# The last block's last matrix product in column halves, on top of product 6's bank; one of its sums on ScalarE and GpSimd

## Chip, cores and metric

One core of one Trainium2 chip runs the whole program. The metric is device time in microseconds (us). The kernel before takes 217.72 us, the median of three runs (217.53 to 218.18).

## What is computed

```python
scores = (1 / sqrt(64)) * q @ k.T            # batch 4, heads 8, 768 positions, head size 64
keep   = (pos_k < 4) | (0 <= pos_q - pos_k < 128)   # 4 sink positions and a window of 128
a      = softmax(where(keep, scores, -1e9))
x      = (a @ v).reshape(3072, 512)          # tokens x model
h      = x @ w_in                            # 512 -> 2048
g      = h * sigmoid(1.702 * h)
out    = g @ w_out                           # 2048 -> 512, float32, 3072 x 512
```

## The kernel before

The 3072 tokens are worked in 12 blocks of 256 (`k` = 0 to 11, `NK` = 12). For each block TensorE makes the attention scores, ScalarE their exponentials, VectorE the mask and the normalised rows; then `mm1` (from line 824) multiplies by `w_in` (line 843), ScalarE takes a tanh (line 857) and VectorE makes `gT` from it (line 859). The last matrix product of a block is in `mm2_seven` (from line 880). It runs for blocks 1 to 11 and replaces the eight products of a 2 by 2 split (128 tokens, half of the 2048, 256 output columns) by seven, with sums of `gT` parts in `sm` (line 890) and of `w_out` parts in `wt` (line 873). Each product is eight matmuls of 256 columns, one for each 128 of its half of the 2048 (line 920).

The four output quarters are `c11`, `c12` (first 128 tokens, left and right 256 columns; tile `osb2` in the last block) and `c21`, `c22` (second 128 tokens; tile `osb3`). With P1 to P7 for the seven products, the sums are c11 = P1 + P2, c12 = P1 + P6 + P5 + P3, c21 = P1 + P7 + P4 + P6 and c22 = P1 + P7 + P6 + P5, each times 0.5. A product lands in a PSUM bank; where the next product is added to it in the bank, it runs with `start=False`. `read` (line 942) takes a bank out: on ScalarE as a copy times 0.5 (line 945), on VectorE as 0.5 times the bank plus an `osb` quarter (line 947).

The last block (`k == NK - 1`, lines 952 to 975) has its own order: P1 in bank a, copied by ScalarE to c12; P7 in bank e, added by VectorE to c22; P2 on top of P1, copied by ScalarE to c11; P4 on top of P7, added to c21; P6 in bank b, which VectorE reads three times (c12, c21, c22); P5 in bank d, read twice (c12, c22); P3 in a bank of its own, f, read once (c12). Each finished quarter leaves by a DMA of 128 KB from SyncE's queue (line 973): c11, c21, c22, c12.

The order is not that of the source. Every step is an `Op` with a cost, the steps that it depends on and a priority. `Plan.run` (line 70) goes through a model of the engines with these costs, and then writes the instructions out in the order of the planned starts. Semaphore waits are put in afterwards, from the tiles that an instruction reads and writes; for a PSUM bank such a wait can be for any earlier user of that bank. Each engine works its own instructions strictly in order.

Of the kernel before, what the change touches and what calls it, by code (L numbers as in the profile page):

```python
# [9 lines left out]
FP32 = mybir.dt.float32  # L10
FP16 = mybir.dt.float16
AF = mybir.ActivationFunctionType
ALU = mybir.AluOpType

P = 128
D = 64
TB = 256
# [37 lines left out]
class Plan:  # L55
# [4 lines left out]
    def op(self, eng, dur, lat, fn, deps=(), prio=0.0, acq=None, rel=(), kind=""):  # L60
        return self.any({eng: (dur, lat)}, lambda _: fn(), deps, prio, acq, rel, kind)
# [138 lines left out]
def pe_ns(n):  # L200
    return n / 2.4 + 2.5
# [3 lines left out]
def kernel(  # L205
# [11 lines left out]
    nc = tc.nc  # L217
# [28 lines left out]
    HM = d_model // 2  # L246
# [4 lines left out]
    def ring(name, n, shape, dt):  # L251
        return [pool.tile(list(shape), dt, name=f"{name}{i}") for i in range(n)]
# [19 lines left out]
    at = ring("at", RA, (P, 2, 512), FP16)  # L272
# [4 lines left out]
    th = ring("th", RTH, (P, 512), FP16)  # L277
    gT = ring("gT", RG, (P, NF, TB), FP16)
    sm = ring("sm", RSM, (P, 4, NH, P), FP16)
    osb = ring("osb", RO, (P, d_model), FP32)  # L280
# [3 lines left out]
    op = plan.op  # L284

    def f32(o, i=0):
        return bank[o.banks[i]]
# [21 lines left out]
    def uses(name, slot, o):  # L309
        users.setdefault((name, slot), []).append(o)  # L310

    def reuse(name, slot):

        return users.pop((name, slot), [])
# [23 lines left out]
    def keep_sinks():  # L338
# [9 lines left out]
        out=bias, in0=mask, scalar1=-1.0, scalar2=-OUT, op0=ALU.add, op1=ALU.mult), [o_mask], prio=MASK_AT, kind="mask")  # L348
# [8 lines left out]
    for b in range(B):  # L357
# [7 lines left out]
        prio = 24000.0 + 300.0 * b if b else NEVER + 0.5  # L365
# [46 lines left out]
    def nominal(k, slot):  # L412
        return 9000.0 + k * L + slot * L / 8
# [466 lines left out]
    def mm2_seven(k):  # L880


        g, X = gT[k % RG], sm[k % RSM]
        A = {"11": g[:, 0:NH, 0:P], "12": g[:, NH:NF, 0:P], "21": g[:, 0:NH, P:TB], "22": g[:, NH:NF, P:TB]}
        lo, hi = [o_g[k, s] for s in range(NS // 2)], [o_g[k, s] for s in range(NS // 2, NS)]
        war = reuse("sm", k % RSM)
        prio = nominal(k + 1, 0)

        def add(n, out, x, y, alu, deps):
            o = op("DVE", 595, 690, lambda: nc.vector.tensor_tensor(out=out, in0=x, in1=y, op=alu),  # L890
                   deps, prio=prio, kind="sum")
            uses("gT", k % RG, o)
            return o

        o1 = add("1", X[:, 0], A["21"], A["22"], ALU.add, lo + hi + war)
        o2 = add("2", X[:, 1], X[:, 0], A["11"], ALU.subtract, [o1] + war)
        o3 = add("3", X[:, 2], A["11"], A["21"], ALU.subtract, lo + war)
        o4 = add("4", X[:, 3], A["12"], X[:, 1], ALU.subtract, [o2] + war)
        S1, S2, S3, S4 = (X[:, n] for n in range(4))
        prod = {1: (A["11"], wq["11"], lo, None), 2: (A["12"], wq["21"], hi, None), 3: (S4, wq["22"], [o4], None),  # L900
                4: (A["22"], wt["4"], hi, "4"), 5: (S1, wt["1"], [o1], "1"), 6: (S2, wt["2"], [o2], "2"),
                7: (S3, wt["3"], [o3], "3")}
        O, wars = [], []
        for j in range(2):
            oi = n_o[0] % RO
            n_o[0] += 1
            O.append(oi)
            wars.append(reuse("osb", oi))
        T = [osb[oi] for oi in O]
        c11, c12, c21, c22 = T[0][:, 0:HM], T[0][:, HM:], T[1][:, 0:HM], T[1][:, HM:]  # L910
        last = {}

        def mm(n, slot, bank_of, first, after=()):

            x, w, deps, t = prod[n]
            for h in range(2):
                F0 = 4 * h
                def f(F0=F0, h=h):
                    for Fi in range(F0, F0 + 4):
                        nc.tensor.matmul(f32(holder[bank_of])[:, 0:HM], x[:, Fi], w[:, Fi],  # L920
                                         start=first and Fi == 0, stop=Fi == NH - 1,
                                         skip_group_check=True)
                d = list(deps) if t or n == 3 else deps[2 * h : 2 * h + 2]
                if k == SEVEN_FROM:
                    d = d + [*o_wout.values()]
                if t:
                    d = d + [o_wt[t, 2 * h], o_wt[t, 2 * h + 1]]
                d = d + list(after) + ([last[bank_of]] if bank_of in last else [])
                begin = first and h == 0
                o = op("PE", 4 * pe_ns(HM), 3 * pe_ns(HM) + HM / 2.4 + 166, f, d,  # L930
                       prio=nominal(k + 1, slot + h / 2 + -1) + 3, acq=("s" if k == NK - 1 else "o", 1) if begin else None,
                       kind="mm2")
                if begin:
                    holder[bank_of] = o
                last[bank_of] = o
                o_P[k, n, h] = o
                uses("gT", k % RG, o)
                uses("sm", k % RSM, o)

        holder = {}  # L940

        def read(eng, bank_of, out, add, deps, end, slot):
            src = lambda: f32(holder[bank_of])[:, 0:HM]
            if eng == "ACT":
                f, ns = (lambda: nc.scalar.mul(out, src(), 0.5)), (264, 380)  # L945
            else:
                f, ns = (lambda: nc.vector.scalar_tensor_tensor(  # L947
                    out=out, in0=src(), scalar=0.5, in1=add, op0=ALU.mult, op1=ALU.add)), (333, 425)
            return op(eng, *ns, f, [last[bank_of]] + deps, prio=nominal(k + 1, slot) + 3,
                      rel=[(holder[bank_of], 0)] if end else [], kind="read")  # L950

        if k == NK - 1:

            mm(1, 0, "a", True)
            r1 = read("ACT", "a", c12, None, wars[0], False, 1)
            mm(7, 1, "e", True)
            r7 = read("DVE", "e", c22, c12, [r1] + wars[1], False, 2)
            mm(2, 2, "a", False, [r1])
            ends = [(0, 0, read("ACT", "a", c11, None, wars[0], True, 3))]
            mm(4, 3, "e", False, [r7])  # L960
            r4 = read("DVE", "e", c21, c12, [r1] + wars[1], True, 4)
            mm(6, 4, "b", True)
            r6 = read("DVE", "b", c12, c12, [r4, r7], False, 5)
            ends.append((1, 0, read("DVE", "b", c21, c21, [r4], False, 5)))
            r26 = read("DVE", "b", c22, c22, [r7], True, 5)
            mm(5, 5, "d", True)
            ends.append((1, HM, read("DVE", "d", c22, c22, [r26], False, 6)))
            r5 = read("DVE", "d", c12, c12, [r6], True, 6)
            mm(3, 6, "f", True)
            ends.append((0, HM, read("DVE", "f", c12, c12, [r5], True, 7)))  # L970
            for j, c, after in ends:
                def f(j=j, c=c):
                    nc.sync.dma_start(out[k * TB + j * P : k * TB + j * P + P, c : c + HM], T[j][:, c : c + HM])
                uses("osb", O[j], op("SP", 500, (400.0,), f, [after], prio=nominal(k + 1, 7) + 4, kind="out"))
            return
        mm(1, 0, "a", True)
        r1 = read("ACT", "a", c21, None, wars[1], False, 1)
        mm(6, 1, "b", True)
        mm(2, 2, "a", False, [r1])
        r11 = read("ACT", "a", c11, None, wars[0], True, 3)  # L980
        r2 = read("DVE", "b", c12, c21, [r1] + wars[0], False, 2)
        mm(7, 3, "b", False, [r2])
        r3 = read("DVE", "b", c22, c21, [r1] + wars[1], False, 4)
        mm(5, 4, "d", True)
        mm(4, 5, "b", False, [r3])
        r22 = read("DVE", "d", c22, c22, [r3], False, 5)
        r21 = read("DVE", "b", c21, c21, [r1, r2, r3], True, 6)
        mm(3, 6, "d", False, [r22])
        r12 = read("DVE", "d", c12, c12, [r2], True, 7)
        prio = nominal(k + 1, 7) + 4  # L990
        for j, after in ((1, [r21, r22]), (0, [r11, r12])):
            rows = out[k * TB + j * P : k * TB + j * P + P, :]
            paired = rows.rearrange("(p i) f -> i p f", i=2)
            for i in range(2):
                def f(to=paired[i], fr=T[j][64 * i : 64 * i + 64], i=i):
                    nc.sync.dma_start(to, fr)
                o_d = op("SP", 500, (400.0,), f, after, prio=prio, kind="out")
                uses("osb", O[j], o_d)

    def mm2(k):  # L1000
        if SEVEN_FROM <= k < SEVEN_TO:
            return mm2_seven(k)
# [127 lines left out]
```

## Time and profile before

| | |
|---|---|
| time, median of three runs | 217.72 us (217.53 to 218.18) |
| time of the profiled execution | 218.23 us |
| its span, first to last instruction | 216.2 us |
| granted TensorE clock | 1.00 |
| TensorE busy | 210.8 us, 97% |
| VectorE busy | 185.4 us, 86% |
| ScalarE busy | 133.1 us, 62% |
| GpSimd busy | 86.0 us, 40% |
| last matmul ends | 213.09 us |
| last VectorE instruction ends | 213.55 us |
| last output bytes move | until about 214.97 us |

The profile is of one execution, so its times are compared with its own 218.23 us: 2.03 us of that lie outside the span. PE is TensorE's matmuls, PEld its weight loads, DVE VectorE, ACT ScalarE, POOL GpSimd, SP SyncE; SPq and ACTq are the sequencers that issue DMAs. Matmul ends are modelled. A row "x8" in the timeline is eight instructions of one group, from the start of the first to the end of the last.

### The profile page before, as it was taken

To read this page: it belongs to the slowest core of one execution; us is meant where nothing else is said; L and a number is where in the kernel's file an instruction comes from. 1 tells how busy PE (TensorE), PEld (TensorE's weight loads), DVE (VectorE), ACT (ScalarE), POOL (GpSimd) and SP (SyncE) were. 2 spreads that over 40 slices of the span, in tenths; PEclk is the share of its full clock that TensorE was granted. 3 is DMA by queue.
4 is the path that set the end of the run, shared out by engine and by line. 5 is a ranking of instruction groups with operands and counts; after the bars stand their busy time and mean duration, and the time that the engine had idled before them with its cause. 6 is when DMAs were issued, how large, how long until landed. Compare 5 with 4: busy or idle time off the path is not lost.

```text
span 216.2 us, 6592 instructions
## 1 busy us (share of the span) xinstructions
PE 210.8 (97%) x2680; PEld 181.0 (84%) x2680; DVE 185.4 (86%) x429; ACT 133.1 (62%) x277; POOL 86.0 (40%) x136
## 2 busy tenths in 40 slices
PE   7899999999999999999999999999999999999994
PEld 7568887678888988988888988888889889888883
DVE  5698899998988988988988979889979879878674
ACT  3867695366686775765675775864675865744330
POOL 7979564499996260699300080540000000000000
PEclk9999999999999999999999999999999999999999
DMA  6999999999999498099970099091040031022042
GB/s 179 215 196 179 200 192 205 168 163 166 108 167 165 30 144 77 5 133 170 89 124 3 0 96 125 5 114 36 3 97 3 0 76 28 0 52 49 2 100 97
DMA packets 79734, 21.41 MB, mean 99 GB/s; under 512 B 68184, under 2 KB 76888, under 8 KB 79704
## 3 DMA queue, kind: packets, MB, share of 16 engines
q0 software_dynamic: 71200, 12.59, 73.2%
q1 hardware_dynamic: 7416, 7.88, 13.5%
q10 hardware_dynamic: 1088, 0.52, 0.8%
q8 instruction: 21, 0.34, 0.7%
q14 instruction: 9, 0.07, 0.1%
HBM read 27.26 MB, written 6.29 MB: 155 GB/s over the span
## 4 chain that ended last, share of the span: by engine, by line
PE 92%; DVE 3%; DMA 2%; ACTq 1%; issue 0%
PE bank L843 39%; PE bank L920 31%; PE bank L695 5%; PE bank L775 5%; PE bank L1021 3%; DMA qk<-in_k_dram 2%; PE bank L618 2%; PE bank L770 2%; PE bank L585 2%; PE bank L555 1%; DVE osb L947 1%; PE bank L642 1%; PE bank L803 1%; ACTq L505 1%; PE bank L678 1%; DVE xn L792 1%
## 5 line engine op out<-in xcount | busy, mean ns | idle before, releaser
L843 PE MATMUL bank<-xT,w_in 128*128 128x256 f16 x768 | 103.7, 273 | 0.0
L857 ACT ACTIVATE th<-bank 128x512 f16<-128x512 f32 x96 | 57.6, 604 | 57.9 <-PE bank L843 51.6
L843 PEld LDWEIGHTS <-w_in 128*128 128x128 f16 x768 | 71.9, 98 | 8.9
L859 DVE SCALAR_TENSOR_TENSOR gT<-th,bank 128x512 f16<-128x512 f16 x96 | 64.9, 678 | 10.1 <-ACT th L857 9.8
L724 ACT ACTIVATE at<-bank 128x512 f16<-128x512 f32 (+1 forms) x96 | 49.1, 584 | 1.5 <-PE bank L695 1.1
L458 POOL DMA_DIRECT2D v<-in_v_dram x48 | 33.2, 719 | 30.4 <-PE bank L775 24.8
L920 PEld LDWEIGHTS <-sm 128*128 128x128 f16 x352 | 33.3, 98 | 4.2 <-issue 0.2
L920 PE MATMUL bank<-wt,sm 128*128 128x256 f16 x264 | 36.1, 273 | 0.0
L947 DVE SCALAR_TENSOR_TENSOR osb<-bank,osb 128x256 f32<-128x256 f32 x58 | 23.9, 417 | 11.8 <-PE bank L920 11.8
L920 PEld LDWEIGHTS <-gT 128*128 128x128 f16 x264 | 25.5, 98 | 3.4
L920 PE MATMUL bank<-w_out,gT 128*128 128x256 f16 x176 | 26.1, 273 | 0.0
L738 DVE TENSOR_TENSOR at<-at,mask 128x1024 f16<-128x1024 f16 x30 | 20.5, 683 | 0.2 <-ACT at L724 0.2
L792 DVE TENSOR_TENSOR xn<-bank,rcp 128x256 f16<-128x256 f32 x48 | 20.0, 417 | 0.6
L775 PE MATMUL bank<-v,at 128*128 128x65 f16 x352 | 20.0, 193 | 0.0
L434 POOL DMA_DIRECT2D qk<-in_q_dram x20 | 18.0, 925 | 0.6 <-DMA qk<-in_q_dram 0.5
L434 POOL DMA_DIRECT2D qk<-in_k_dram x20 | 18.0, 923 | 0.7 <-PE bank L843 0.5
L775 PEld LDWEIGHTS <-at 128*128 128x128 f16 x352 | 17.4, 97 | 0.9
L305 POOL COPY ks<-qkT 64x4 f16<-64x4 f16 x26 | 8.1, 313 | 18.6 <-DVE qkT L305 17.6
L890 DVE TENSOR_TENSOR sm<-gT 128x1024 f16<-128x1024 f16 x22 | 15.0, 680 | 0.1
L593 ACT ACTIVATE ats<-bank 128x256 f16<-128x256 f32 x32 | 13.0, 405 | 1.7 <-PE bank L585 1.6
L945 ACT ACTIVATE osb<-bank 128x256 f32<-128x256 f32 x22 | 8.4, 382 | 9.1 <-PE bank L920 9.1
L695 PE MATMUL bank<-qkT 64*128 64x256 f16 x192 | 13.3, 244 | 0.0
(58 smaller groups left out, 224.0 us busy)
## 6 DMA issues: line engine op xcount, KB each, us to landing
out_dram<-osb SPq DMA_DIRECT2D x48, 128.0 KB
v<-in_v_dram POOLq DMA_DIRECT2D x48, 64.0 KB, 5.1
qk<-in_q_dram POOLq DMA_DIRECT2D x20, 128.0 KB, 5.4
qk<-in_k_dram POOLq DMA_DIRECT2D x20, 128.0 KB, 5.6
w_out<-in_moe_w_out_dram POOLq DMA_DIRECT2D x4, 512.0 KB, 11.3
w_in<-in_moe_w_in_dram POOLq DMA_DIRECT2D x4, 256.0 KB, 6.6
w_in<-in_moe_w_in_dram POOLq DMA_DIRECT2D x2, 512.0 KB, 8.9
qk<-in_k_dram ACTq DMA_DIRECT2D x4, 128.0 KB
```

Of the source, the lines that this page charges most:

```text
L434: nc.gpsimd.dma_start(c16[:, i, e, hs], src[b, hs, t0 : t0 + TB].rearrange("h (p i) d -> i p h d", i=2)[i])
L458: o = op("POOL", ISSUE, (430 if k < 2 else V_NS,), lambda i=i, j=j, src=src: nc.gpsimd.dma_start(w16[64 * i : 64 * i + 64, j, :, 0:D], src ...
L695: nc.tensor.matmul(f32(o_b or o_s, 2 * n + i)[:, c : c + w].rearrange("s (j t) -> s j t", t=P), src[d, j, 1, p], T[d, j0:j1, 0, p], start= ...
L724: nc.scalar.activation(out=A[:, i, 0:W], in_=f32(o_b or o_s, 2 * n + i)[:, 0:W], func=AF.Exp, scale=scale)
L738: nc.vector.tensor_tensor(out=a_, in0=a_, in1=m_[:, 2 * P :].unsqueeze(1).to_broadcast((P, 4, 2 * P)), op=ALU.mult,)
L775: nc.tensor.matmul(avp()[:, j, i], A[:, i, c : c + P], src[:, jj, 2 * p + i, 0:E], start=not r and n == 0, stop=n == len(blocks) - 1, skip ...
L792: o_nn = op("DVE", 333, 425, lambda: nc.vector.tensor_tensor(out=X[:, p].rearrange("s j (h d) -> s j h d", h=2), in0=avp()[:, :, :, 0:D], ...
L843: nc.tensor.matmul(f32(holder[0])[:, bass.ts(e, TB)], w_in16[:, c, bass.ts(Fi, P)], X[:, c], start=(c == 0 and not (halved and e)), stop=( ...
L857: o_t = op("ACT", 477, 600, lambda first=first: nc.scalar.activation(out=th[first.places[0]], in_=f32(first), func=AF.Tanh, scale=0.851), ...
L859: o_g[k, s] = op("DVE", 595, 690, lambda first=first, s=s: nc.vector.scalar_tensor_tensor(out=g[:, 2 * s : 2 * s + 2].rearrange("p a t -> ...
L920: nc.tensor.matmul(f32(holder[bank_of])[:, 0:HM], x[:, Fi], w[:, Fi], start=first and Fi == 0, stop=Fi == NH - 1, skip_group_check=True)
L947: f, ns = (lambda: nc.vector.scalar_tensor_tensor(out=out, in0=src(), scalar=0.5, in1=add, op0=ALU.mult, op1=ALU.add)), (333, 425)
```

## The change

Only the last block changes. `mm` and `read` get a column offset `at` and a width `w_`.

- Bank b (P6) is read once by VectorE, for c21 (`r6`), and once by ScalarE, which copies it times 0.5 to a spare float32 tile in the space of `th0` (`r16`). GpSimd adds that tile to c22 (`a6`). The read of P6 into c12 is gone.
- VectorE reads bank d (P5) first into c12, then into c22; the second comes after GpSimd's add.
- P3 no longer has a bank. It runs on top of P6 in bank b, left 128 columns and then right 128 columns: sixteen matmuls of 128 columns in place of eight of 256. VectorE reads each half, 128 columns, into c12, which holds P1 + P5 by then.
- c12 leaves in two DMAs of 64 KB, the left half from ScalarE's queue and the right half from SyncE's.

```diff
-            r6 = read("DVE", "b", c12, c12, [r4, r7], False, 5)
-            ends.append((1, 0, read("DVE", "b", c21, c21, [r4], False, 5)))
-            r26 = read("DVE", "b", c22, c22, [r7], True, 5)
+            r6 = read("DVE", "b", c21, c21, [r4], False, 5)
+            ends.append((1, 0, HM, r6))
+
+            spare = th[0][:].bitcast(FP32)[:, 0:HM]
+            r16 = read("ACT", "b", spare, None, [], False, 5)
+            a6 = op("POOL", 420, 540, lambda: nc.gpsimd.tensor_tensor(out=c22, in0=c22, in1=spare, op=ALU.add),
+                    [r7, r16], prio=nominal(k + 1, 5) + 3, kind="read")
             mm(5, 5, "d", True)
-            ends.append((1, HM, read("DVE", "d", c22, c22, [r26], False, 6)))
-            r5 = read("DVE", "d", c12, c12, [r6], True, 6)
-            mm(3, 6, "f", True)
-            ends.append((0, HM, read("DVE", "f", c12, c12, [r5], True, 7)))
-            for j, c, after in ends:
-                def f(j=j, c=c):
-                    nc.sync.dma_start(out[k * TB + j * P : k * TB + j * P + P, c : c + HM], T[j][:, c : c + HM])
-                uses("osb", O[j], op("SP", 500, (400.0,), f, [after], prio=nominal(k + 1, 7) + 4, kind="out"))
+            r5 = read("DVE", "d", c12, c12, [r4, r7], False, 6)
+            ends.append((1, HM, HM, read("DVE", "d", c22, c22, [a6], True, 6)))
+
+            w_ = HM // 2
+            for h in range(2):
+                mm(3, 6 + h, "b", False, [r6, r16], at=h * w_, w_=w_)
+                to = c12[:, h * w_ : h * w_ + w_]
+                ends.append((0, HM + h * w_, w_, read("DVE", "b", to, to, [r5], bool(h), 7 + h, h * w_, w_)))
+            for j, c, w_, after in ends:
+                eng = "ACT" if (j, c) == (0, HM) else "SP"
+                def f(j=j, c=c, w_=w_, dma=nc.scalar if eng == "ACT" else nc.sync):
+                    dma.dma_start(out[k * TB + j * P : k * TB + j * P + P, c : c + w_], T[j][:, c : c + w_])
+                uses("osb", O[j], op(eng, 500, (400.0,), f, [after], prio=nominal(k + 1, 7) + 4, kind="out"))
```

In the changed program the instructions of every engine stand as before up to product 6 of the last block. Behind it they are, with the semaphore each waits for:

- VectorE: c21 from bank b (waits for P6); c12 from bank d (P5); c22 from bank d (GpSimd's add); the left half of c12, and the right half, from bank b. The left half's wait is for a TensorE count that only the last of the sixteen matmuls raises; the right half has no wait of its own.
- ScalarE: the copy of bank b to the spare tile waits for VectorE's c21 read; the DMA of the left half waits for VectorE's left half.
- GpSimd: the add waits for ScalarE's copy.
- TensorE: the first of the sixteen matmuls waits for ScalarE's copy.
- SyncE: DMAs of c11, c21, c22, and the right half of c12.

More of the change, by code (lines that the diff above doesn't have):

```diff
@@ L911, in mm2_seven, with mm @@
         last = {}
-        def mm(n, slot, bank_of, first, after=()):
+        def mm(n, slot, bank_of, first, after=(), at=0, w_=HM):
             x, w, deps, t = prod[n]
@@ L919, in f @@
                     for Fi in range(F0, F0 + 4):
-                        nc.tensor.matmul(f32(holder[bank_of])[:, 0:HM], x[:, Fi], w[:, Fi],
+                        nc.tensor.matmul(f32(holder[bank_of])[:, at : at + w_], x[:, Fi], w[:, Fi, at : at + w_],
                                          start=first and Fi == 0, stop=Fi == NH - 1,
@@ L929, in mm @@
                 begin = first and h == 0
-                o = op("PE", 4 * pe_ns(HM), 3 * pe_ns(HM) + HM / 2.4 + 166, f, d,
+                o = op("PE", 4 * pe_ns(w_), 3 * pe_ns(w_) + w_ / 2.4 + 166, f, d,
                        prio=nominal(k + 1, slot + h / 2 + -1) + 3, acq=("s" if k == NK - 1 else "o", 1) if begin else None,
@@ L940, in mm2_seven, with read @@
         holder = {}
-        def read(eng, bank_of, out, add, deps, end, slot):
-            src = lambda: f32(holder[bank_of])[:, 0:HM]
+        def read(eng, bank_of, out, add, deps, end, slot, at=0, w_=HM):
+            src = lambda: f32(holder[bank_of])[:, at : at + w_]
             if eng == "ACT":
@@ L947, in read @@
                 f, ns = (lambda: nc.vector.scalar_tensor_tensor(
-                    out=out, in0=src(), scalar=0.5, in1=add, op0=ALU.mult, op1=ALU.add)), (333, 425)
+                    out=out, in0=src(), scalar=0.5, in1=add, op0=ALU.mult, op1=ALU.add)), (66 + w_ / 0.96, 158 + w_ / 0.96)
             return op(eng, *ns, f, [last[bank_of]] + deps, prio=nominal(k + 1, slot) + 3,
@@ L958, in mm2_seven @@
             mm(2, 2, "a", False, [r1])
-            ends = [(0, 0, read("ACT", "a", c11, None, wars[0], True, 3))]
+            ends = [(0, 0, HM, read("ACT", "a", c11, None, wars[0], True, 3))]
             mm(4, 3, "e", False, [r7])
```

## The prediction

> **What bounds the kernel now.** I read the chain of work that ended last on the profile's page, then the timeline of the last 6 us, then the stretches behind the last instruction. The chain by engine is this line:
>
> ```profile
> PE 92%; DVE 3%; DMA 2%; ACTq 1%; issue 0%
> ```
>
> TensorE sets the pace throughout. The change touches only what follows product 6 of the last block, so its price is read there. The chain of waits near the end, start and length in us, and the timeline:
>
> ```profile
> 211.35 0.03 issue
> 211.38 0.48 DVE osb L947 x2
> 211.86 0.19 issue
> 212.05 1.50 DVE osb L947 x4
> ```
>
> ```profile
> 210.30 1.91 PE L920 MATMUL bank<-wt,sm 128*128 128x256 f16 x16
> ...
> 211.38 2.17 DVE L947 SCALAR_TENSOR_TENSOR osb<-bank,osb 128x256 f32<-128x256 f32 x6 [0.34 <-PE bank L920]
> 212.05 1.04 PE L920 MATMUL bank<-w_out,sm 128*128 128x256 f16 x8
> ```
>
> The sixteen matmuls are P6 and P5: 0.109 us apart and 0.273 each, so P6 ends at 210.30 + 7 x 0.109 + 0.273 = 211.34 and P5 at 212.21. P3 ends at 213.09. Six VectorE reads follow P6, 0.33 apart (211.38, 211.72, 212.05, 212.38, 212.71), the last at 213.13, 0.04 after P3; it ends at 213.55. VectorE could have taken it at 213.04, so P3 and VectorE bind almost alike. SyncE issues c21 at 212.16, c22 at 213.15 and c12 at 213.58, each 0.02 to 0.03 behind its read.
>
> Behind that only transfers run (columns: stretch, its length, busy time of PE, PEld, DVE, ACT, POOL, clock, DMA share, GB/s):
>
> ```profile
> 213.50:213.75 0.25, 0.00 (x0) 0.00 (x0) 0.05 (x1) 0.00 (x0) 0.00 (x0) 1.00 0.00 0
> 213.75:214.00 0.25, 0.00 (x0) 0.00 (x0) 0.00 (x0) 0.00 (x0) 0.00 (x0) 1.00 0.04 16
> 214.00:214.25 0.25, 0.00 (x0) 0.00 (x0) 0.00 (x0) 0.00 (x0) 0.00 (x0) 1.00 0.88 307
> 214.25:214.50 0.25, 0.00 (x0) 0.00 (x0) 0.00 (x0) 0.00 (x0) 0.00 (x0) 1.00 0.71 230
> 214.50:214.75 0.25, 0.00 (x0) 0.00 (x0) 0.00 (x0) 0.00 (x0) 0.00 (x0) 1.00 0.89 320
> 214.75:215.00 0.25, 0.00 (x0) 0.00 (x0) 0.00 (x0) 0.00 (x0) 0.00 (x0) 1.00 0.52 176
> ```
>
> The reader is to see that c22 and c12 move almost back to back, 256 KB from 214.0 to 214.97: 0.85 us from issue to first bytes, 0.45 to 0.48 per 128 KB. The span ends 1.23 later; that tail is common to both kernels.
>
> **The change part by part**, on this execution's clock.
>
> *Leaving:* VectorE's read of P6 into c12 and the one into c22, 0.33 each. c21 is then read first, at 211.38, and its DMA goes 0.34 earlier; nothing waits for that.
>
> *ScalarE's copy of bank b* waits for the c21 read, not only for P6. That read ends at 211.38 + 0.42 = 211.80. A wait of ScalarE on VectorE cost 0.03 (a VectorE copy ends at 5.64, ScalarE starts at 5.67). The copy has a row:
>
> ```profile
> L945 ACT ACTIVATE osb<-bank 128x256 f32<-128x256 f32 x22 | 8.4, 382 | 9.1 <-PE bank L920 9.1
> L1089 PE MATMUL bank<-zero 128*128 128x128 f16 x72 | 6.5, 261 | 1.1 <-DVE zero L321 1.1
> L305 POOL CAST qk<-qk 128x512 f16<-128x512 f32 x1 | 0.6, 600 | 1.2 <-DMA qk<-in_k_dram 1.2
> L335 POOL TENSOR_SCALAR_AFFINE_SELECT mask<-mask 64x256 f16<-64x256 f16 x4 | 1.7, 420 | 0.7 <-DVE mask L343 0.5
> ```
>
> So it runs from 211.83 to 212.21. ScalarE is otherwise idle here.
>
> *Product 3 waits for that copy*, since it writes on top of P6. TensorE is woken 0.06 after its releaser (VectorE's copy ends at 13.01, the matmul starts at 13.07): it starts at 212.27, not at 212.05, a new stall of 0.22. Nothing is queued behind it on TensorE; its readers, VectorE's two narrow reads and the last two DMAs, all wait.
>
> *Sixteen matmuls of 128 columns.* Their pace has a row in the start-up, at full clock: sixteen 128x128 matmuls, each with a weight load, take 1.07 us from 10.15 to 11.22, so (1.07 - 0.26) / 15 = 0.054 apart. The upper bound is the weight load's own 0.098. I take 0.054, as weight loads lie beside matmuls everywhere in this trace. With 0.22 for the last one (the transposes of 128 columns, line 803, last 221 ns) P3 takes 15 x 0.054 + 0.22 = 1.03, ends at 213.30, and costs nothing by itself: eight wide ones take 1.04.
>
> The Trainium skill speaks against this step: "TensorE: Matmul & The Clock Gate", section "Back-to-back issue gap", gives about 81 ns per matmul for a sustained stream of weight load and 128-column matmul. By it P3 would end 15 x 0.027 = 0.41 later, an estimate; the start-up row above has 54 ns and speaks against the page.
>
> *GpSimd's add* waits for ScalarE's copy. GpSimd starts 0.07 after its releaser (VectorE's memset ends at 1.82, GpSimd starts at 1.89), here at 212.28. No two-input GpSimd operation is in the trace. From below: 256 columns of the cast's rate, 600 / 512 x 256 = 0.30 us. From above: three passes (two inputs, one output) at the mask rows' slope, 420 against 286 ns for 256 and 128 columns (1.05 ns a column, 0.15 fixed), 3 x 0.27 + 0.15 = 0.96. I take 0.65: the two inputs read one after the other, 512 columns, at the cast's rate (0.60) or at the mask rows' (0.15 + 2 x 0.27 = 0.69). It ends at 212.93.
>
> *VectorE.* c12 from P5 runs at 212.26, beside GpSimd's add. c22 waits for the add: 0.05 later, 212.98 to 213.40. It stands ahead of the two narrow reads, which can start from 213.31. A column costs 1.02 ns ((678 - 417) / 256 from the rows of lines 859 and 947), so a read of 128 columns lasts 0.42 - 0.13 = 0.29 and lets the next one start after 0.20. The left half is not read while the right half is computed: its wait is for the last of the sixteen matmuls. So it starts at 213.34 and the right half at 213.54, ending at 213.83, 0.28 later than before. If GpSimd took over 0.68, c22 would hold up both halves and every further 0.1 would cost 0.1.
>
> *Transfers.* SyncE issues c22 at 213.42 (0.27 later), ScalarE the left half at 213.66, SyncE the right half at 213.85 (0.27 later than c12). With the same 0.85, c22's bytes start at 214.27 and the halves are due at 214.51 and 214.70, before c22's 0.45 is over. So 256 KB run in one piece, as before: until 215.17 (2 x 0.45) to 215.24 (0.97). Packets of 512 bytes do not slow it: the start-up loads have them and move 300 GB/s. ScalarE's queue may be slower to issue (0.49 against 0.46 in the loads); up to 0.2 of that hides behind c22's bytes.
>
> **Sum.** Wait for ScalarE +0.22, narrower last read -0.13, second narrow read +0.20, narrower matmuls -0.01: the last read ends 0.28 later. The smaller last DMA (-0.22) would take nearly all of that back, but c22's transfer, 0.27 later behind GpSimd, keeps the queue full, so the last bytes move about 0.2 later. The span becomes 216.4, the profiled time 218.43, and on the median **217.9 us**: 0.1% slower, which counts as the same (about 0.3%, 0.65 us, is what a measurement of this kernel can tell from no change).
>
> **The rivals.**
>
> 1. *Nothing lost.* GpSimd's add is as quick as the lower bound: c22 is read from 212.63, its DMA goes at 213.07, and the last bytes are the right half's, due at 214.70 and done at 214.92, so -0.05; less delay in the new waits would bring -0.2. 217.6. For it: the cast row. Against it: the add reads two operands. The Trainium skill, "DMA: Bandwidth & Descriptors", section "Issuing engines are not separate DMA queues", says that a second queue saves issue time alone; no run here shows two queues storing at once. If the second queue moved bytes beside the first at full rate, the end would be this rival's even with a slow add.
>
> 2. *Slower: GpSimd's add becomes the end.* c22's read blocks VectorE's queue from 0.68 us on. For +0.65 the add needs about 1.1 us: c22's read from 213.43, its DMA at 213.87, 256 KB from 214.72 to 215.62 or later. 218.4 or more. Against it: that is above my three-pass bound. A lock between VectorE and GpSimd could bring it near, and the trace has one, but not for this read: a GpSimd copy of 0.18 passes beside line 947 and takes 0.65 beside line 890.
>
> ```profile
> 88.29 0.42 DVE L947 SCALAR_TENSOR_TENSOR osb<-bank,osb 128x256 f32<-128x256 f32 x1
> ...
> 88.46 0.18 POOL L305 COPY ks<-qkT 64x4 f16<-64x4 f16 x1
> ...
> 88.63 0.68 DVE L890 TENSOR_TENSOR sm<-gT 128x1024 f16<-128x1024 f16 x1
> ```
>
> 3. *Weight loads pace the narrow matmuls.* At 0.098 P3 ends at 213.96, the right half at 214.49, the last bytes at about 215.6: +0.6, 218.3. At the page's figure the same sum gives +0.35, an estimate.
>
> 4. *The change would do all that it says:* the left half is read and sent while the right half is computed. The program's wait excludes it; without it, c22 still bars VectorE until 213.31, so it would give no more than 0.03, so it stays inside the forecast.
>
> **Chances.** My forecast (+0.05 to +0.45) 0.58; rival 1 0.20; rival 2 0.10; rival 3 0.07; a gain above 0.65 us, for which I find no mechanism, 0.05. Rivals 2 and 3 are slower by over 0.3% in most of their cases (0.14 with the edge of the forecast). So faster 0.05, same 0.81, slower 0.14. The bounds are -0.2 (rival 1) and +0.6 (rival 3, or the add at 0.96, which gives +0.5); with 0.1 of scatter, 217.4 to 218.5.
>
> **What would show it.** In the profile after: ScalarE's line 945 at 211.8, TensorE idle for 0.2 before sixteen matmuls of 128 columns 54 ns apart, the add at about 0.65 us on GpSimd, c22's read directly behind it, both narrow reads behind the last matmul, and output bytes without a gap until 215.2. Wrong would be: an add under 0.45 or over 0.9, a matmul pace near 0.1, or bytes of the left half moving before c22's.

## The result, and the profile after

The changed kernel takes 219.09 us (median of 8 runs, 218.66 to 220.18) against 218.04 for the kernel before, run beside it: ratio 1.0054, 95% interval 1.0036 to 1.0071. It is slower: the medians lie 1.05 us apart, and the ratio stands for 1.18. The forecast was 217.9, in a range of 217.4 to 218.5.

The profiled execution took 219.28 us with a span of 217.48, against 218.23 and 216.25. Of the 1.23 us between the spans, 0.34 arise ahead of the change: product 6 of the last block starts at 210.64 and not at 210.30. Its start lies anywhere from 209.9 to 210.9 in the profiles used below, one for each kernel, of kernels that are all but the same up to there, so this part is taken for scatter. Behind it the trace repeats within about 0.02 us, and there the change costs 0.90 us: from product 6's start to the end of the span 6.84 us, 5.95 before. All times "behind product 6" below are counted from that start, in each kernel's own trace.

The timeline of the changed kernel from product 6's end on (start, length, engine, line, what):

```profile
211.71 0.42 DVE L947 SCALAR_TENSOR_TENSOR osb<-bank,osb 128x256 f32<-128x256 f32 x1 [0.34 <-PE bank L920]
...
212.23 0.38 ACT L945 ACTIVATE th<-bank 128x256 f32<-128x256 f32 x1 [1.89 <-DVE osb L947]
212.59 0.42 DVE L947 SCALAR_TENSOR_TENSOR osb<-bank,osb 128x256 f32<-128x256 f32 x1 [0.45 <-PE bank L920]
212.66 1.05 PE L920 MATMUL bank<-w_out,sm 128*128 128x128 f16 x16
...
212.75 0.73 POOL L968 TENSOR_TENSOR osb<-osb,th 128x256 f32<-128x256 f32 x1 [69.21 <-ACT th L945]
213.51 0.82 DVE L947 SCALAR_TENSOR_TENSOR osb<-bank,osb 128x256 f32<-128x256 f32 x3 [0.50 <-POOL osb L968]
```

The order is the one forecast: c21's read, ScalarE's copy, GpSimd's add, c22's read, the two halves. c21's read starts 1.07 behind product 6, where the forecast had 1.08; each step behind it is later than forecast. The output bytes, in the same columns as before:

```profile
214.50:214.75 0.25, 0.00 (x0) 0.00 (x0) 0.00 (x0) 0.00 (x0) 0.00 (x0) 1.00 0.00 0
214.75:215.00 0.25, 0.00 (x0) 0.00 (x0) 0.00 (x0) 0.00 (x0) 0.00 (x0) 1.00 0.71 242
215.00:215.25 0.25, 0.00 (x0) 0.00 (x0) 0.00 (x0) 0.00 (x0) 0.00 (x0) 1.00 0.98 318
215.25:215.50 0.25, 0.00 (x0) 0.00 (x0) 0.00 (x0) 0.00 (x0) 0.00 (x0) 1.00 0.90 285
215.50:215.75 0.25, 0.00 (x0) 0.00 (x0) 0.00 (x0) 0.00 (x0) 0.00 (x0) 1.00 0.67 203
215.75:216.00 0.25, 0.00 (x0) 0.00 (x0) 0.00 (x0) 0.00 (x0) 0.00 (x0) 1.00 0.01 2
```

One piece, as forecast. But from its end, 215.78, to the end of the span it is 1.71 us, where the kernel before has 1.25 (its bytes end at 215.00, and not at the 214.97 given above). That 0.46 us lies in SyncE's closing waits. At the end of the program SyncE waits for every DMA semaphore in turn and then drains. The instructions of the program's last line on SyncE's sequencer, from the last landing to the drain (count, ns of one, first and last start), first before and then after. A landing is taken here as the start of the wait instruction that the transfer releases, 0.02 behind the transfer's last semaphore update:

```profile
L1125 SPq DRAIN  x2: 7/10/13, 215.4 to 215.5; - x2
L1125 SPq EVENT_SEMAPHORE  x1: 28/28/28, 215.4 to 215.4; - x1
```

```profile
L1134 SPq EVENT_SEMAPHORE  x8: 27/28/28, 216.2 to 216.6; - x8
L1134 SPq DRAIN  x1: 13/13/13, 216.7 to 216.7; - x1
```

Before, the last landing (5.06 behind product 6) ends the last wait of the list, and the drain follows 0.07 later. After, the last landing (5.52) ends a wait near the list's head. The seven that follow have long been satisfied, but each takes its turn, 0.062 us apart, and the drain comes 0.50 after the landing. The eight completion semaphores of SyncE's and ScalarE's DMAs are handed out in turn over the whole program. The last block now has five DMAs, not four, so its last one gets number 0, which the list names first of the eight; before it had number 7, named last.

So the theory, A: 0.46 us because the last bytes land later, and 0.43 because the last DMA's semaphore stands early in the list. The rivals: B, that halves land late (rows of 512 bytes, ScalarE's queue); C, that all of it is the later last read and GpSimd's add; D, called E in a later experiment, that product 3's new wait for ScalarE is the cause of the later landing.

### The profile page after: what moved, and what is told of

Read it like the earlier page. It is cut to its first block, busy times and chain, and to the rows that moved or that the text cites. A ratio compares the mean times of both kernels' runs of the same rounds, so it can differ in the third digit from the quotient of the medians.

```text
span 217.5 us, 6613 instructions
## 1 busy us (share of the span) xinstructions
PE 211.4 (97%) x2688; PEld 181.8 (84%) x2688; DVE 184.9 (85%) x428; ACT 133.6 (61%) x278; POOL 86.5 (40%) x137
## 4 chain that ended last, share of the span: by engine, by line
PE 90%; DMA 3%; POOL 2%; DVE 1%; issue 0%; POOLq 0%; ACT 0%; SPq 0%; DVEq 0%; ACTq 0%
PE bank L843 39%; PE bank L920 31%; PE bank L695 5%; PE bank L775 5%; DMA qk<-in_k_dram 3%; PE bank L1030 3%; PE bank L618 2%; PE bank L770 2%; PE bank L585 2%; POOL v L458 1%; PE bank L555 1%; PE bank L642 1%; POOL mask L335 1%; PE bank L803 1%; DVE osb L947 0%
## 5 line engine op out<-in xcount | busy, mean ns | idle before, releaser
L947 DVE SCALAR_TENSOR_TENSOR osb<-bank,osb 128x256 f32<-128x256 f32 (+1 forms) x57 | 23.3, 412 | 12.8 <-PE bank L920 12.2
L968 POOL TENSOR_TENSOR osb<-osb,th 128x256 f32<-128x256 f32 x1 | 0.7, 726 | 69.2 <-ACT th L945 69.2
```

The costliest lines, as they stand in the source:

```text
L947: f, ns = (lambda: nc.vector.scalar_tensor_tensor(out=out, in0=src(), scalar=0.5, in1=add, op0=ALU.mult, op1=ALU.add)), (66 + w_ / 0.96, 1 ...
```

## Experiments

What each measured behind product 6 (us from its profile) and by its times:

| kernel | last landing | landing to drain | end of span | ratio to before (95%) |
|---|---|---|---|---|
| before | 5.06 | 0.07 | 5.95 | |
| changed | 5.52 | 0.50 | 6.84 | 1.0054 (1.0036 to 1.0071) |
| before, c11 in two DMAs | 5.08 | 0.50 | 6.39 | 1.0024 (1.0010 to 1.0038) |
| changed, c11 in eight DMAs | 6.07 | 0.07 | 6.96 | 1.0029 (1.0012 to 1.0046) |
| changed, c12 in one DMA | 5.54 | 0.07 | 6.42 | 1.0010 (0.9995 to 1.0024) |
| changed, without GpSimd | 5.14 | 0.49 | 6.45 | 1.0011 (0.9996 to 1.0026) |
| changed, other semaphore | 5.52 | 0.07 | 6.42 | 1.0006 (0.9993 to 1.0020) |
| before, the sum alone | 5.53 | 0.07 | 6.42 | 1.0004 (0.9982 to 1.0027) |
| before, the halves alone | 5.04 | 0.07 | 5.93 | 1.0002 (0.9985 to 1.0019) |
| candidate, sum into c12 | 5.37 | 0.07 | 6.26 | 1.0014 (1.0001 to 1.0027) |
| changed, ScalarE first | 5.22 | 0.07 | 6.12 | 0.9992 (0.9975 to 1.0010) |
| candidate, c22 early | 5.09 | 0.07 | 5.99 | 0.9984 (0.9964 to 1.0003) |
| before, semaphore in the middle | 5.06 | 0.31 | 6.19 | 0.9991 (0.9976 to 1.0007) |

A quarter of a microsecond is 0.11%, less than most of these intervals are wide, and the scatter ahead of product 6 is larger. So the columns from the profiles decide, each from one execution, and the ratios only where they are wide apart. Clear of 1 are the intervals of the changed kernel, of c11 in two and in eight DMAs and, barely, of the sum into c12.

The two do not agree everywhere. Eight of the twelve ratios lie 0.12% to 0.20% below what the columns give, and two intervals leave the columns' value out: with the other semaphore in the changed kernel (0.47 us would be 1.0022) and with the semaphore in the middle (0.24 us would be 1.0011). Part of this lies outside the span. The time less the span is 1.70 to 1.75 us in seven of the eight kernels (median of their runs) and 1.85 to 1.92 in the kernel before run beside them. That is 0.05% to 0.10%; why it differs, and where the rest lies, is open. The cut of a transfer in block 4, described below, does not mark these kernels: four of the eight have it, and two kernels that have it too fit their columns. Three of theory A's expected ratios (c12 in one DMA, without GpSimd, other semaphore) lie above their intervals; they fit a start from the changed kernel's 1.0054, which itself is 0.13% above its columns.

**c11 in two DMAs, in the kernel before.** Each piece has 128 / `n` rows and a DMA of its own. This moves the semaphore of the last DMA and, near the end, nothing else. Dots in the cuts stand for lines left out.

```diff
...
+                n = 2 if (j, c) == (0, 0) else 1
...
```

> The kernel before with one edit: c11's transfer is cut into two of 64 rows each, so the last block has five output DMAs and the last one (c12) gets another completion semaphore, one that SyncE's closing list of waits names second instead of last. Theory A (the order of SyncE's closing waits costs the time): output bytes end as before, but eight further waits come after the last landing, about 0.05 us each, so the run is 0.4 to 0.5 us slower than before, ratio about 1.002. Rival B (the late end comes from ScalarE's queue or from 512-byte rows landing late): no difference, as neither is in this kernel. Rival C (all of the loss is the later last read and the GpSimd add): no difference.

From the last landing to the drain, on SyncE's sequencer:

```profile
L1128 SPq EVENT_SEMAPHORE  x8: 28/28/28, 215.5 to 216.0; - x8
L1128 SPq DRAIN  x1: 7/7/7, 216.0 to 216.0; - x1
```

The landing is where it was (5.08), the drain comes 0.50 later, and the kernel is 0.24% slower with no halves, no add on GpSimd and no output on a second queue in it. The last DMA's wait is the first of the list's eight, with seven behind it, not the second with eight as expected. A holds. B and C each expected nothing here.

**c11 in eight DMAs, in the changed kernel.** Meant to bring the last DMA back to semaphore 7.

```diff
...
+                n = 8 if (j, c) == (0, 0) else 1
...
```

> The changed kernel with one edit: c11's transfer is cut into eight of 16 rows, which puts the last DMA (right half of c12) on the semaphore that SyncE's closing list names last. Theory A: 0.4 to 0.5 us faster than the changed kernel, ratio to before about 1.003. Rival B: the same as the changed kernel (ratio 1.005), as the halves still go in 512-byte rows on two queues. Rival C: the same as the changed kernel.

The closing part does fall from 0.50 to 0.07. But the eight issues take 0.46 us each of SyncE's sequencer and hold up c22's and c12's: the landing moves to 6.07 and the span behind product 6 gains nothing. The experiment was badly built. Its ratio, 1.0029, is the one expected, but by luck: the columns would give 1.0046. The one with the other semaphore, below, replaces it.

**c12 whole, in the changed kernel.**

```diff
-                ends.append((0, HM + h * w_, w_, read("DVE", "b", to, to, [r5], bool(h), 7 + h, h * w_, w_)))
+                last_read = read("DVE", "b", to, to, [r5], bool(h), 7 + h, h * w_, w_)
+            ends.append((0, HM, HM, last_read))
-                eng = "ACT" if (j, c) == (0, HM) else "SP"
+                eng = "SP"
```

> The changed kernel with c12 sent whole in one DMA of 128 KB from SyncE's queue behind the second narrow read: four output DMAs, the last on the semaphore named last. Theory A: the closing waits are as before (0.45 us back), bytes end within 0.1 us of the changed kernel's, because the 256 KB of c22 and c12 still run in one piece behind c22; ratio to before about 1.003. Rival B: likewise about 0.45 us faster, so this run alone does not part A from B, but it gives the worth of splitting c12 once the waits are equal. Rival C: slower than the changed kernel by up to 0.2 us, since the last transfer is twice as long.

The landing is at 5.54, against 5.52 with two halves on two queues: sending by halves is worth 0.02 us here, since c22's bytes and c12's run in one piece either way. The Trainium skill, "DMA: Bandwidth & Descriptors", section "Issuing engines are not separate DMA queues", says that a second issuing engine saves the time of issuing alone; the 0.02 us agree.

**Without GpSimd, in the changed kernel.**

```diff
-            spare = th[0][:].bitcast(FP32)[:, 0:HM]
-            r16 = read("ACT", "b", spare, None, [], False, 5)
-            a6 = op("POOL", 420, 540, lambda: nc.gpsimd.tensor_tensor(out=c22, in0=c22, in1=spare, op=ALU.add),
-                    [r7, r16], prio=nominal(k + 1, 5) + 3, kind="read")
+            a6 = r16 = read("DVE", "b", c22, c22, [r7], False, 5)
```

> The changed kernel without ScalarE's copy and GpSimd's add: VectorE reads product 6 into c22 straight from its bank, as before. The two halves of product 3 on top of product 6, their two reads and their two queues stay, and so does the last semaphore. Theory A: product 3 starts behind VectorE's second read of the bank, 0.1 us later or earlier than in the changed kernel; c22 is read 0.4 us earlier, so output bytes end 0.2 to 0.35 us earlier; the closing waits stay. Ratio to before about 1.003 to 1.004. Rival B: the same, since queue and rows stay. Rival C (the add is the whole loss): 0.9 us faster than the changed kernel, ratio 1.000.

The landing comes 0.38 earlier, slightly more than expected, and is only 0.08 behind the kernel before. The closing waits stay at 0.49. C expected all of the loss gone; the profile leaves 0.50. The ratio, 1.0011, does not part the two: it is nearer to C's 1.000, and A's 1.003 to 1.004 lie above its interval.

**Another semaphore, in the changed kernel.** One output transfer of block 4, far from the end, is cut into eight DMAs of 8 rows each, which shifts all later semaphores by seven.

```diff
             for i in range(2):
...
+                n = 8 if (k, j, i) == (4, 1, 0) else 1
...
```

> The changed kernel with one edit far from the end: one output transfer of block 4 is cut into eight, which moves the completion semaphores of all later DMAs on by seven, so that the right half of c12 gets the one that SyncE's closing list names last. Nothing in the last block is moved, unlike in the run with c11 cut into eight, where the pieces held up SyncE's last two issues. Theory A: 0.4 to 0.5 us faster than the changed kernel, ratio to before about 1.003; from the last landing to SyncE's drain 0.07 us in place of 0.50. Rival B (late landing by ScalarE's queue or 512-byte rows): as the changed kernel, 1.005.

Every instruction of the last block stands where it stood behind product 6 (copy 1.59, add 2.11, halves 3.21 and 3.41, landing 5.52), and the span shrinks by 0.43, to 6.42. B expected no change; its ratio of 1.005 lies above the interval, as A's 1.003 does. Between this and the first experiment the position is shown from both sides.

**The sum alone, in the kernel before.** Product 3 keeps its bank, width and single DMA. VectorE reads product 6 for c21 first and then for c12.

```diff
...
-            r26 = read("DVE", "b", c22, c22, [r7], True, 5)
+            r6 = read("DVE", "b", c21, c21, [r4], False, 5)
...
+            r6b = read("DVE", "b", c12, c12, [r4, r7], False, 5)
...
+            r16 = read("ACT", "b", spare, None, [], True, 5)
+            a6 = op("POOL", 420, 540, lambda: nc.gpsimd.tensor_tensor(out=c22, in0=c22, in1=spare, op=ALU.add),
+                    [r7, r16], prio=nominal(k + 1, 5) + 3, kind="read")
...
```

> The kernel before with only the sum moved: ScalarE copies bank b, GpSimd adds it to c22; product 3 keeps its own bank, its 256 columns, its one read and one DMA. Four output DMAs, so the closing waits are as before. Theory A: c22's read waits for GpSimd until about 2.9 us behind the start of product 6, and the last landing is 0.4 to 0.5 us later than before although product 3 never waits: ratio 1.002. Rival D (the new wait of product 3 for ScalarE's copy is what moves the landing): no more than 0.1 us.

Its timeline:

```profile
211.80 0.38 ACT L945 ACTIVATE th<-bank 128x256 f32<-128x256 f32 x1 [1.89 <-DVE osb L947]
211.95 1.04 PE L920 MATMUL bank<-w_out,sm 128*128 128x256 f16 x8
212.21 1.62 DVE L947 SCALAR_TENSOR_TENSOR osb<-bank,osb 128x256 f32<-128x256 f32 x4 [0.51 <-ACT th L945]
212.32 0.72 POOL L968 TENSOR_TENSOR osb<-osb,th 128x256 f32<-128x256 f32 x1 [69.20 <-ACT th L945]
```

TensorE does not wait (product 3 starts 1.75 behind product 6, as before), and still the landing is at 5.53: the sum alone makes the whole later landing. As in the changed kernel, c22's read starts at 2.87 to 2.88, behind GpSimd's add, and SyncE issues c22 at 3.32 and its last DMA at 3.75. D falls. The ratio, 1.0004 with an interval to 1.0027, neither shows nor excludes the 0.47 us.

**The halves alone, in the kernel before**, in two banks of their own, with the cut in block 4.

```diff
-            mm(3, 6, "f", True)
...
+            for h in range(2):
+                n_ = "fg"[h]
+                mm(3, 6 + h, n_, True, at=h * w_, w_=w_)
+                to = c12[:, h * w_ : h * w_ + w_]
+                ends.append((0, HM + h * w_, w_, read("DVE", n_, to, to, [r5], True, 7 + h, h * w_, w_)))
...
```

> The kernel before with only the halves: product 3 by column halves in two banks of its own, read and sent by halves on two queues; all of product 6's reads stay on VectorE. One output transfer of block 4 is cut into eight, so that the closing waits are as before. Theory A: the halves by themselves change the landing by -0.05 to 0, as c22's transfer, unchanged, keeps the DMA engines busy until the halves are due: ratio 1.000. Rival B: 0.3 to 0.5 us slower.

Landing 5.04, span 5.93: 0.02 better than before. As the two halves lie in different banks, the left one is read (2.74) before the right one's matmuls end (2.80), and still it brings no more: c22's bytes and both halves run in one piece.

**A candidate: the sum into c12, ScalarE first.**

```diff
...
+            r16 = read("ACT", "b", spare, None, [], False, 4)
+            a6 = op("POOL", 730, 850, lambda: nc.gpsimd.tensor_tensor(out=c12, in0=c12, in1=spare, op=ALU.add),
...
```

> A candidate made from the theory: ScalarE copies bank b first, as soon as product 6 ends; GpSimd adds it to c12, which is needed last, and not to c22; VectorE reads product 6 for c21 and c22, then finishes c22, then c12; product 3 by halves in two banks of its own; the last DMA on the semaphore named last. Theory A: c22 leaves 0.2 us earlier than before, last landing 0.15 to 0.3 us earlier than before, ratio 0.999. Rival: GpSimd's add ends after 2.4 us behind product 6's start, and c12 is held up: no gain, 1.000.

It is slower than before by 0.31, so the expectation and its rival both missed. The add ends at 2.32, in time; but c22's second read (2.35) then waits for c22's first (ends 2.25), and the left half (3.21) for c12's read just ahead of it (ends 3.10). Both times the read adds to the quarter that the instruction right in front of it writes, and starts 0.10 after that one has ended; reads of different quarters overlap and start 0.33 apart.

**ScalarE's copy first, in the changed kernel**, with the cut in block 4. It was run twice: the ratio is the first's, the profile shown that of the second, a single execution of 218.58 us. The first's profile has nearly the same end, 6.10 behind product 6.

```diff
-            r6 = read("DVE", "b", c21, c21, [r4], False, 5)
+            r16 = read("ACT", "b", spare, None, [], False, 4)
+            r6 = read("DVE", "b", c21, c21, [r4, r16], False, 5)
...
```

> The changed kernel with the last DMA on the semaphore named last (as in the run with block 4's transfer cut) and one reordering: ScalarE's copy of bank b goes ahead of VectorE's c21 read instead of behind it, so the chain copy, add, c22 read starts 0.52 us earlier; c21 starts 0.42 later, and product 3 waits for it. Theory A (what is left of the loss is this chain): c22's read starts near 2.35 us behind product 6's start (2.87 in the changed kernel, 2.41 in the kernel before), the span behind product 6 comes to within 0.1 us of the kernel before, ratio 1.000. Rival E (product 3's start behind ScalarE is the loss): product 3 still starts 0.2 us late, so at least 0.2 us of the loss stays, ratio 1.001 or more.

> The kernel with ScalarE's copy first once more, for a profile of it: the span behind product 6's start again 6.10 us (5.95 before, 6.42 with VectorE first), product 3 again 0.22 us late, last landing at 5.2 us, set by product 3's second half and no longer by c22.

```profile
211.57 0.38 ACT L945 ACTIVATE th<-bank 128x256 f32<-128x256 f32 x1 [1.37 <-PE bank L920]
...
212.09 0.73 POOL L967 TENSOR_TENSOR osb<-osb,th 128x256 f32<-128x256 f32 x1 [68.68 <-DMA out_dram<-osb]
212.46 1.05 PE L920 MATMUL bank<-w_out,sm 128*128 128x128 f16 x16
213.55 0.49 DVE L947 SCALAR_TENSOR_TENSOR osb<-bank,osb 128x128 f32<-128x128 f32 x2 [0.28 <-PE bank L920]
```

Product 6 starts at 210.49 here. c22's read moves up by half a microsecond (2.36 behind product 6) and the landing by 0.30, to 5.22. It does not get back to 5.06: product 3 still starts 0.22 late, its last read ends 3.55, its DMA is issued at 3.58 and lands 1.64 later. So E is right for what is left: 0.16 us behind the larger chain. A's expected ratio of 1.000 was met by the time, but its 0.1 us on the span was missed by 0.07.

**A candidate without GpSimd, c22 early**: the halves as above, and VectorE's reads in the order c22, c12, c21 (product 6), c22, c12 (product 5), halves.

> A candidate without GpSimd: product 3 by halves in two banks of its own, read and sent by halves on two queues, the last DMA on the semaphore named last, and VectorE's reads in an order that finishes c22 earlier: product 6 into c22, c12, c21, then product 5 into c22, c12, then the halves. Theory A: c22 leaves 0.33 us earlier than before, the last read ends 0.1 to 0.2 later, and the last landing is 0.05 to 0.15 us earlier than before, ratio 0.9995, too little to part from no change by the times; the span behind product 6 shows it. Rival: the left half waits for c12's read just ahead of it, and the landing is not earlier.

Landing 5.09, no gain, where 0.05 to 0.15 us was expected. c22's landing does come earlier (4.41 against 4.57), but the left half waits for c12's read right ahead of it (ends 2.82, starts 2.93), as the rival said; the right half is issued at 3.44 and lands 1.65 later. No version here beats the kernel before by more than the 0.02 us of the halves alone.

**The semaphore in the middle, in the kernel before.** The dose: block 4's transfer cut into five, so four waits stand behind the last DMA's.

```diff
...
+                n = 5 if (k, j, i) == (4, 1, 0) else 1
...
```

> The kernel before with one output transfer of block 4 cut into five, and nothing else: the last DMA's completion semaphore moves on by four, to the middle of SyncE's closing list, with four of the list's waits behind it. Theory A, as a dose: from the last landing to SyncE's drain 0.07 + 4 x 0.062 = 0.31 us, where the kernel before has 0.07 and the changed one 0.50; the span behind product 6's start 0.25 us longer than before. If the position in the list costs nothing: 0.07 and no change.

```profile
L1128 SPq EVENT_SEMAPHORE  x5: 27/28/28, 215.9 to 216.2; - x5
L1128 SPq DRAIN  x2: 7/7/7, 216.3 to 216.3; - x2
```

0.31 from landing to drain, span behind product 6 longer by 0.24: both as expected, though the times do not show it. Three positions (0, 3 and 7 of eight) give 0.50, 0.31 and 0.07.

## Why the prediction was wrong

**The step that failed is "The span ends 1.23 later; that tail is common to both kernels."** It is not: it has the closing waits in it. The change adds one DMA, the last DMA's semaphore moves to the front of the list, and 0.43 us come behind the last landing. The trace of before could have told it: SyncE's closing list took 0.06 us a wait there too, seven in a row while c22's bytes were still under way, where they cost nothing:

```profile
L1125 SPq EVENT_SEMAPHORE  x7: 28/28/28, 214.0 to 214.4; - x7
```

I named the output DMAs one by one and did not ask which semaphore each gets.

**The second cause is a size.** The landing was forecast 0.2 us later and came 0.46 later. Counted behind product 6, with the forecast in brackets: ScalarE's copy starts 1.59 (1.53), as it came 0.09 behind the read and not 0.03; GpSimd's add starts 2.11 (1.98), 0.14 behind the copy and not 0.07; it takes 0.73 (0.65); c22 is read from 2.87 (2.68), the halves from 3.21 and 3.41 (3.04 and 3.24), the last DMA is issued at 3.75 (3.55). Two waits of 0.06 to 0.07 more each and 0.08 of the add make the 0.2. The short waits were taken from single places in the start-up, where the copy and GpSimd's instruction carry their wait themselves. In the changed kernel a wait instruction of its own (ACTq, POOLq) stands ahead of each, as the chain of work that ended last shows:

```profile
212.17 0.02 ACTq L945
212.19 0.04 issue
212.23 0.39 ACT th L945
212.62 0.03 POOLq L968
212.65 0.07 issue
```

That these make the difference was not tried.

**What held.** Product 3 waits for ScalarE: a stall of 0.28 against 0.22. The sixteen narrow matmuls take 1.05 us together, 0.056 apart, and cost nothing; rival 3 does not show here. Nor do the 81 ns that the Trainium skill, "TensorE: Matmul & The Clock Gate", section "Back-to-back issue gap", gives for a sustained stream. The left half's read waits for a count that only the last of the sixteen raises (rival 4), though it was c22's read that it started behind. c22 did bar VectorE, as the add passed the 0.68 us from which it would: the left half could have been read at 3.12 and was read at 3.21. The bytes ran in one piece. The chain of ScalarE's copy and GpSimd's add is the cause of the later landing, as rival 2 had it for the add, but at 0.73 us the add stays under the 1.1 that this rival needed. Rival 1 (nothing lost) is out. None of the signs that the prediction named for being wrong appeared: none of them looked at the end of the program.

**The sum as it is:** 0.47 for the sum on ScalarE and GpSimd (alone: 6.42 - 5.95), 0.43 for the place of the last semaphore (6.845 - 6.417), about 0 for the halves and for product 3's wait while c22 is later still: 0.90, all that the profile shows behind product 6. The medians differ by 1.05. The remaining 0.15 is less than the scatter ahead of product 6, and the interval (0.8 to 1.5 us) holds 0.90. The split into 0.47 and 0.43 rests on the profiles: the times put the semaphore alone at 0.2 to 0.8 us (c11 in two DMAs) and the sum alone anywhere from 0.4 faster to 0.6 slower. Against the number on record, a part is also that the kernel before has a median of 218.04 in eight runs and 217.72 in the three shown.

## What to carry to other kernels

When a change alters the number of DMAs, look at which completion semaphore the last one gets and where the program's closing list of waits names it: a satisfied wait is cheap but not free, and those behind the last landing are paid in full. A sum moved from VectorE (0.33 us of its time) to ScalarE and GpSimd costs here a chain of three waits between engines and two instructions (1.37 us from the end of c21's read to the start of c22's); it pays only where nothing needs the result for that long. And halving the last transfer brought 0.02 us here, with an earlier transfer still in front of it.

## What the runs showed of the hardware that was not expected

- A wait on SyncE that is already satisfied takes 0.062 us of its sequencer: seven behind the last landing took 0.43 us.
- The start of one instruction after another engine's end was not one constant: ScalarE behind VectorE 0.09 us (0.03 in the start-up), GpSimd behind ScalarE 0.14, the first behind 69 idle microseconds; TensorE behind ScalarE 0.05.
- GpSimd's add of two 128x256 float32 tiles takes 0.73 us, in every kernel that has it, beside VectorE's reads.
- A DMA of 64 KB that ends the program lands 1.64 to 1.65 us after its issue where c22's bytes are out of its way, and 1.77 behind them. One of 128 KB takes 1.78 behind c22's bytes (c12 before), and about 1.73 with nothing in front (c21 before). So half the bytes save about 0.1 us, where the prediction's sum had 0.22 for it.
